# The sign of the weights from ScalarE's scaling, and their scale from Gram products: one change to an attention and FFN kernel

## The chip, the cores and the metric

The kernel runs on one NeuronCore of one Trainium2 chip. The metric is the device time of one execution in microseconds (us), lower is better; the time given is the median of three runs. Engines are named as in the profile: PE is TensorE (PEld its weight loads), DVE VectorE, ACT ScalarE, POOL GpSimd, SP SyncE, which issues all transfers here.

## What is computed

The reference takes eight batches of eight heads through a local attention (512 positions with a window of 32 to either side, plus 32 global keys and queries), then through a block that mixes with a two-dimensional Fourier transform, normalises, and applies two weight matrices with a ReLU between them:

```python
x = attention(q_l, k_l, v_l, q_g, k_g, v_g)      # 8 x 544 x 512, fp32
X = np.fft.fft(np.fft.fft(x, axis=1), axis=2)
u = x + np.real(X)
un = (u - mean(u)) / np.sqrt(var(u) + 1e-06)
ch = np.maximum(un @ w_ch1, 0.0) @ w_ch2          # 512 x 2048 and 2048 x 512, float64
return (u + ch).astype(np.float32)
```

## The kernel before

Everything in fp32 accuracy is done on PE as three fp16 products of a high and a low part. Work is cut into jobs: each of the 32 head pairs of the attention (four pairs to a batch, four units of 128 query rows to a pair), a Fourier stage for each of eight batches, 17 chunks of 256 rows for the two matrix products, of which the last four run as two pairs with seven products in place of eight. A list scheduler at the foot of the file gives each job an engine, an estimated duration, what it reads and writes, and a due time; among the jobs that are ready on an engine the one due first goes first, and the order so found is written out as fixed instruction streams. Nothing is reordered on the chip. The constants at the head of the file (`T0`, `STEP`, `U_AT`, `S2_AT`, `L_HOLD`, `BOOST` and so on) set the due times, holds and margins of that scheduler, and hence only the order.

The head of the program, some 135 us, holds three things at a time. The first is the weights: 32 blocks of 128 x 512 float64 values (k = 0 for the first matrix, k = 1 for the second, 512 KB each) are loaded and turned to fp32 by integer arithmetic on the two words of each value. `w_low` (L424 on POOL, every fourth on ACT, L422) takes the low word to mantissa bits; `w_split64` (L415, ACT) scales the high word by 2^-112 into PSUM, with buffers for two blocks; `w_size` (L428, DVE) shifts that left by three and joins it with the low bits, which loses the sign; `w_sum` (L438, PE) multiplies the size, taken as bf16, by a matrix of equal constants to sum up sizes by column; `w_sign` (L442, DVE) goes over the block again and joins the sign bit from PSUM. For every four blocks `w_max` (L448 and small operations at L533, L536, L454 to L457, DVE) makes a power-of-two scale from the largest sum. Then `w_hi` (L478, ACT) and `w_lo` (L471, DVE) write the scaled fp16 parts. The second thing is batch 0's attention: scores (L623, PE), masked minimum (L631, DVE), exponential (L638, ACT; L707 for the global queries), high part (L642, ACT), low part (L647, POOL), a transposing transfer `ph` to `pl` (L652, issued on SP), the values (L668 and L671, PE), the norm (L682 to L684, DVE). Batch 1's loads (L510, L514) follow on SP. The third is batch 0's Fourier stage and first normalisation: L830 to L855, L913, L933, L948, L965, L974, L1013 to L1056. Then the first product (`f_first`, L1084) of chunk 0 starts, which waits by its dependence `wend` for the last `w_sum` as well, and the second (`f_second`, L1103), which needs the scaled second matrix. From there chunks run while the attention of the next batches is prepared beside them.

## Time and profile before

| | us |
|---|---|
| median of three runs | 1009.96 (1007.2 to 1011.59) |
| span of the profiled execution, first to last instruction | 1005.8 |
| PE busy | 917.0 (91%) |
| DVE busy | 753.8 (75%) |
| ACT busy | 629.3 (63%) |
| POOL busy | 581.8 (58%) |

The profiled execution's own time is not listed apart from its span; the three runs are. The span lies 4.2 us under their median and 1.4 us under the fastest, and that remainder is what lies around the span. Busy times are unions over an engine's instructions, so 91% for PE is a mean over a head in which PE mostly waits and a long stretch in which it never does.

### The profile page before, as it was taken

How to read it: one execution, taken by the hardware profiler on the slowest of the kernel's cores; microseconds unless marked ns; L12 is line 12 of the kernel's file. 1: busy time of each engine (PE TensorE's matmuls, PEld its weight loads, DVE VectorE, ACT ScalarE, POOL GpSimd, SP SyncE). 2: the span in 40 equal slices, each digit the busy share in tenths (PEclk: the TensorE clock that was granted, in tenths of full speed). 3: DMA queues.
4: the chain of work that ended last, by engine and by line, in shares of the span. 5: the costliest groups of instructions: out<-in, count | busy, mean ns of one | idle time of the engine just before them, and what ended most of it. 6: DMA issues, size and time to landing. Idle time of an engine off the chain costs nothing.

```text
span 1005.8 us, 25354 instructions
## 1 busy us (share of the span) xinstructions
PE 917.0 (91%) x9784; PEld 644.1 (64%) x9784; DVE 753.8 (75%) x1928; ACT 629.3 (63%) x1361; POOL 581.8 (58%) x861
## 2 busy tenths in 40 slices
PE   1555479999999999999999999999999999999996
PEld 0344366766677677777767677777767766666663
DVE  5998898889858965887678687678775897854543
ACT  6996779976796588857677786676563545411210
POOL 5697378675595478637844774486456199910000
PEclk9999979999999999999999999999999999999998
DMA  9899348626664285537544772574263132201001
GB/s 364 260 241 198 136 110 165 119 96 116 137 153 109 66 178 131 129 60 156 128 86 97 149 159 58 108 131 98 57 122 57 43 72 54 41 8 42 1 2 42
DMA packets 225973, 112.61 MB, mean 112 GB/s; under 512 B 200860, under 2 KB 208444, under 8 KB 225852
## 3 DMA queue, kind: packets, MB, share of 16 engines
q1 hardware_dynamic: 225852, 110.99, 49.0%
q8 instruction: 76, 1.25, 0.5%
q14 instruction: 45, 0.37, 0.1%
HBM read 47.40 MB, written 9.44 MB: 57 GB/s over the span
## 4 chain that ended last, share of the span: by engine, by line
PE 76%; DVE 6%; ACT 1%; issue 1%; DVEq 0%; ACTq 0%
PE acc L1103 24%; PE ps L1084 24%; PE bk L1235 6%; PE ps L1302 4%; PE acc L1302 4%; PE bk L623 4%; PE bk L668 2%; PE bk L671 2%; PE bk L948 2%; PE bk L913 1%; PE bk L695 1%; PE bk L731 1%; DVE xt L985 1%; PE ps L1235 1%; DVE wh L471 1%
## 5 line engine op out<-in xcount | busy, mean ns | idle before, releaser
L1084 PE MATMUL ps<-uh,wh 128*128 128x256 f16 x2496 | 290.2, 274 | 0.4 <-DVE h L1093 0.4
L1103 PE MATMUL acc<-wh,h 128*128 128x512 f16 x1248 | 286.2, 379 | 0.9 <-DVE wh L471 0.7
L1084 PEld LDWEIGHTS <-wh 128*128 128x128 f16 x2496 | 241.2, 98 | 36.7 <-issue 1.3
L1103 PEld LDWEIGHTS <-h 128*128 128x128 f16 x1248 | 117.5, 98 | 128.0 <-issue 1.8
L647 POOL TENSOR_TENSOR ph<-pe,ph 128x448 f16<-128x448 f32 (+1 forms) x128 | 140.7, 1108 | 73.8 <-ACT ph L642 63.1
L1093 DVE SCALAR_TENSOR_TENSOR h<-ps,h 128x512 f16<-128x512 f32 x104 | 71.6, 688 | 87.4 <-ACT h L1089 86.8
L638 ACT ACTIVATE pe<-pe,nm 128x224 f32<-128x224 f32 (+1 forms) x256 | 107.0, 476 | 24.6 <-DVE nm L631 24.3
L1089 ACT ACTIVATE h<-ps 128x512 f16<-128x512 f32 x104 | 61.7, 593 | 89.8 <-PE ps L1084 87.9
L631 DVE CUSTOM_DVE_ANT_0 pe<-bk,msk,z 128x224 f32<-128x224 f32 (+1 forms) x256 | 102.2, 455 | 5.5 <-PE bk L623 5.4
L642 ACT ACTIVATE ph<-pe 128x448 f16<-128x448 f32 (+1 forms) x128 | 73.0, 581 | 8.1 <-DMA pl<-ph 5.9
L668 PE MATMUL bk<-vN,pl 128*128 128x65 f16 x768 | 66.6, 200 | 11.1 <-DMA pl<-ph 11.1
L668 PEld LDWEIGHTS <-pl 128*128 128x128 f16 x768 | 58.7, 102 | 19.2 <-DMA pl<-ph 12.8
L623 PEld LDWEIGHTS <-qT 64*128 64x128 f16 x1536 | 51.0, 98 | 15.8 <-issue 12.8
L623 PE MATMUL bk<-kT,qT 64*128 64x192 f16 (+2 forms) x1536 | 58.1, 221 | 2.9 <-DVE X L684 1.0
L671 PEld LDWEIGHTS <-pl 96*128 96x128 f16 (+1 forms) x768 | 56.7, 102 | 4.7
L438 PE MATMUL wl<-wm,partb 128*128 128x256 bf16 x64 | 18.9, 396 | 44.4 <-DVE wm L428 44.4
L582 POOL TENSOR_TENSOR vN<-vf,vN 128x640 f16<-128x640 f32 x32 | 46.1, 1442 | 21.5 <-ACT vN L578 14.0
L571 POOL TENSOR_TENSOR vf<-vf,z 128x640 f32<-128x640 f32 x32 | 40.8, 1275 | 26.3 <-DVE ge L533 16.2
L607 POOL TENSOR_TENSOR kT<-qk,kT 128x559 f16<-128x559 f32 x32 | 41.6, 1299 | 18.5 <-ACT kT L602 18.2
L1284 ACT ACTIVATE hb<-ph 128x512 f16<-128x512 f32 x16 | 10.1, 631 | 66.4 <-DVE ph L1269 66.4
L671 PE MATMUL bk<-vB,pl 96*128 96x65 f16 (+1 forms) x576 | 50.9, 200 | 0.0
L592 ACT ACTIVATE qk<-qk,z 128x559 f32<-128x559 f32 x64 | 44.3, 728 | 5.4 <-DVE z L533 5.4
(260 smaller groups left out, 1869.3 us busy)
## 6 DMA issues: line engine op xcount, KB each, us to landing
qk<-in_qk SPq DMA_DIRECT2D x32, 535.5 KB, 4.4
rw<-in_moe_w_ch SPq DMA_DIRECT2D x22, 512.0 KB, 6.0
vf<-in_v SPq DMA_DIRECT2D x32, 320.0 KB, 3.2
out<-X SPq DMA_DIRECT2D x13, 512.0 KB, 3.2
raw<-in_moe_w_ch SPq DMA_DIRECT2D x10, 512.0 KB, 4.7
vB<-vN SPq DMA_DIRECT2D x32, 97.5 KB, 2.1
vB<-vN SPq DMA_DIRECT2D x64, 32.5 KB, 1.9
pl<-ph SPq DMA_TRANSPOSE x128, 3.2
```

Source lines behind the costliest of these rows:

```text
L623: nc.tensor.matmul(S[h][:, t + w0:t + w1], qT[r, a, j], kT[r, k0:k0 + w1 - w0], start=m == 0, stop=m == 2)
L631: nc.vector.tensor_tensor_reduce(self.per[j][:, h, 0:w], S[h][:, t:t + w], self.msk[:, j, 0:w], z[:, 8:9], 3e38, op0=ALU.add, op1=ALU.min, ...
L638: self.nc.scalar.activation(pe[:, h], pe[:, h], AF.Exp, bias=nm[:, h:h + 1], scale=-1.0)
L642: self.nc.scalar.activation(ph[:, 0, :, 0:WIDE[i % 4]], self.per[i % 4][:, :, 0:WIDE[i % 4]], AF.Copy)
L647: self.nc.gpsimd.tensor_sub(ph[:, 1, :, 0:w], self.per[i % 4][:, :, 0:w], ph[:, 0, :, 0:w])
L668: nc.tensor.matmul(pv[:, j % 2, h], pl[:, 4 * a + 2 * h], vN[:, j, c, h, :], start=m == 0, stop=False)
L671: nc.tensor.matmul(pv[:, j % 2, h], pl[0:n, 4 * a + 2 * h + 1], vb, start=False, stop=m == 2)
L1084: nc.tensor.matmul(ps[:, q], wt[:, w, c0:c0 + P], uh[:, :, 4 * a + kt, :], start=n == 0, stop=n == 11)
L1093: self.nc.vector.scalar_tensor_tensor(h[:, 1], self.fps.pop((c, fp)), 0.0, h[:, 0], op0=ALU.max, op1=ALU.subtract)
L1103: nc.tensor.matmul(self.acc_f[c][j], h[:, a, q, j * P:(j + 1) * P], self.w[1, f][:, w, :], start=f == 0 and a == 0 and w == 0, stop=f == 1 ...
L1235: nc.tensor.matmul(ps, w[x], a[:, :, k * y + o + kt, :], start=m == 0, stop=m == 5)
L1302: nc.tensor.matmul(self.acc_f[c][j], h[:, a, q, j * P:(j + 1) * P], self.w[1, f][:, w, :], start=first and q + a + w == 0, stop=last and q ...
```

## The change

`w_split64` uses the parametric ReLU with slope -2^32 for negative inputs in place of a copy. A negative high word comes out positive and 2^32 times as large, which adds 32 to its exponent field; after `w_size`'s shift by three that bit stands where the sign belongs. So `w_size` gives the signed value and `w_sign` is gone. The sum of sizes no longer works on signed values, so `w_sum` forms Gram products: each block's four 128-column parts are both the stationary and the moving operand, and the diagonal of the 128 x 128 result holds sums of squares. `w_max` takes the row maximum of 128 columns in place of 256, a new job `w_norm` adds it over partitions by an fp32 product on PE, and a new job `w_scale` makes the power of two by an integer reciprocal root, for every group of four blocks of both matrices. The constants of the scheduler are changed as well.

```diff
+RSQRT = float(0x5F3759DF + (math.log2(600.0) - 6.5) * 2 ** 23)
-T0 = 130.0
-STEP = 5.25
+T0 = 126.448
+STEP = 5.316
-U_AT, U_PACE = 12.0, 4.0
+U_AT, U_PACE = 12.846, 3.951
-W_AT, W_PACE = 4.0, 2.2
-W2_AT, W2_PACE = 54.0, 2.0
-S_AT, S_PACE = 40.0, 3.6
-S2_AT, S2_PACE = 190.0, 3.0
-LDM = 0.8
+W_AT, W_PACE = 4.136, 2.2
+W2_AT, W2_PACE = 54.0, 2.04
+S_AT, S_PACE = 39.185, 3.504
+S2_AT, S2_PACE = 184.602, 2.329
+LDM = 0.778
-PEM, PEM0, SPM = 0.9, 0.6, 0.2
+PEM, PEM0, SPM = 0.737, 0.718, 0.205
-L_HOLD = 70.0
-QUEUE = 2.0
-LOOK_BY = 35.0
-LN, LN1, LN2 = 45.0, 20.0, 50.0
+L_HOLD = 77.65
+QUEUE = 1.933
+LOOK_BY = 31.266
+LN, LN1, LN2 = 41.656, 17.202, 49.261
-PL = 45.0
-T_AT, T_PACE = 800.0, 9.0
-BOOST = 20.0
-BOOST0 = 90.0
+PL = 34.52
+T_AT, T_PACE = 799.979, 10.217
+BOOST = 34.224
+BOOST0 = 82.708
...
-        act.activation(m, self.raw.pop((k, i))[:, :, 1].bitcast(F32), AF.Copy, scale=2.0 ** -112)
+        act.activation(m, self.raw.pop((k, i))[:, :, 1].bitcast(F32), AF.Prelu, scale=2.0 ** -112, alpha=-2.0 ** 32)
...
-            self.wl[k, c] = self.ps.tile([P, 512], F32, name="wl", tag=f"acc{c % 2}")[:, 0:256]
-        b = self.w[k, i].bitcast(BF16).rearrange("p (o n t) -> p o n t", o=2, t=2)
-        for o in range(2):
-            self.nc.tensor.matmul(self.wl[k, c], self.partb, b[:, o, :, 1], start=n + o == 0, stop=n + o == 4)
-
-    def w_sign(self, k, i):
-        w, m = self.wv.pop((k, i))
-        self.nc.vector.scalar_tensor_tensor(w, m.bitcast(I32), -0x80000000, w, op0=ALU.bitwise_and, op1=ALU.bitwise_or)
-        self.w[k, i] = w.bitcast(F32)
+            self.wl[k, c] = self.ps.tile([P, 512], F32, name="wl", tag=f"acc{c % 2}")
+        b = self.w[k, i].bitcast(BF16).rearrange("p (o n t) -> p o n t", o=4, t=2)
+        for o in range(4):
+            self.nc.tensor.matmul(self.wl[k, c][:, 0:P], b[:, o, :, 1], b[:, o, :, 1], start=n + o == 0, stop=n + o == 6)
 
     def w_max(self, k, c):
-        nc, m, w = self.nc, self.mx2, self.wsc
-        v = m[:, c:c + 1]
-        nc.vector.tensor_reduce(v, self.wl.pop((k, c)), axis=EX, op=ALU.max)
-        if k == 0:
-            self.scale_of(w[:, 4 + c:5 + c], v)
-            self.twice_inv(w[:, c:c + 1], w[:, 4 + c:5 + c])
-        elif c == 3:
-            v = m[:, 4:5]
-            nc.vector.scalar_tensor_tensor(m[:, 0:4], m[:, 0:4], 2.0 ** -5, w[:, 0:4], op0=ALU.mult, op1=ALU.mult)
-            nc.vector.tensor_reduce(v, m[:, 0:4], axis=EX, op=ALU.max)
+        self.nc.vector.tensor_reduce(self.mx2[:, 4 * k + c:4 * k + c + 1], self.wl[k, c][:, 0:P], axis=EX, op=ALU.max)
+
+    def w_norm(self, k, c):
+        self.nc.tensor.matmul(self.wl[k, c][:, P:P + 1], self.part, self.mx2[:, 4 * k + c:4 * k + c + 1], start=True, stop=True)
+
+    def w_scale(self, k, c):
+        ve, m, w = self.nc.vector, self.mx2, self.wsc
+        v, r = self.wl.pop((k, c))[:, P:P + 1].bitcast(I32), (w[:, 4 + c:5 + c] if k == 0 else m[:, 4 + c:5 + c])
+        ve.tensor_scalar(r.bitcast(I32), v, -0.5, RSQRT, op0=ALU.mult, op1=ALU.add)
+        ve.tensor_scalar(r.bitcast(I32), r.bitcast(I32), EXPO, None, op0=ALU.bitwise_and)
+        self.twice_inv(w[:, c:c + 1] if k == 0 else r, r)
+        if k and c == 3:
+            v, m = m[:, 8:9], m[:, 4:8]
+            ve.scalar_tensor_tensor(m, m, 2.0 ** -5, w[:, 0:4], op0=ALU.mult, op1=ALU.mult)
+            ve.tensor_reduce(v, m, axis=EX, op=ALU.max)
             self.scale_of(w[:, 13:14], v)
-            nc.vector.tensor_scalar_mul(w[:, 8:12], w[:, 0:4], w[:, 13:14])
+            ve.tensor_scalar_mul(w[:, 8:12], w[:, 0:4], w[:, 13:14])
             self.twice_inv(w[:, 14:15], w[:, 13:14])
...
-            add("DVE", .66, self.w_sign, k, i, r=[m, w], w=[w], t=T + 2)
             if t % 4 == 3:
                 d = [("ws", 0, x) for x in range(4)] + [("ws", 1, x) for x in range(3)] if (k, c) == (1, 3) else []
-                add("DVE", .65 if k == 0 else .35 if c < 3 else 1.25, self.w_max, k, c, r=[wl] + d, w=[("ws", k, c)], t=T + 6)
+                wm = ("wm", k, c)
+                add("DVE", .27, self.w_max, k, c, r=[wl], w=[wm], t=T + 5)
+                add("PE", .3, self.w_norm, k, c, r=[wm], w=[wl], t=T + 5.5)
+                add("DVE", .5 if c < 3 or k == 0 else 1.4, self.w_scale, k, c, r=[wl] + d, w=[("ws", k, c)], t=T + 6)
```

## Rows read from the trace of the kernel before

**Rows 1.** The page: busy tenths in 40 slices of 25 us, by engine.
```profile
PE   1555479999999999999999999999999999999996
DVE  5998898889858965887678687678775897854543
```
**Rows 2.** Windows by stage: busy us (instructions) by engine, granted clock, DMA share, GB/s.
```profile
20.00:77.00 57.00, 29.63 (x375) 20.33 (x373) 54.21 (x133) 54.75 (x111) 46.45 (x55) 1.00 0.91 262
77.00:107.00 30.00, 14.47 (x214) 10.17 (x210) 25.59 (x64) 19.41 (x47) 20.39 (x28) 1.00 1.02 235
107.00:136.00 29.00, 13.15 (x128) 10.14 (x128) 26.65 (x70) 22.85 (x48) 12.46 (x27) 0.81 0.23 76
136.00:176.00 40.00, 38.92 (x480) 28.88 (x478) 35.85 (x92) 33.44 (x70) 32.69 (x42) 0.96 0.69 147
176.00:800.00 624.00, 622.41 (x7272) 444.22 (x7269) 479.88 (x1305) 432.24 (x955) 386.99 (x585) 1.00 0.54 111
800.00:996.00 196.00, 195.24 (x1317) 128.57 (x1315) 122.60 (x241) 55.52 (x110) 73.20 (x106) 1.00 0.13 31
...
200.00:300.00 100.00, 98.65 (x1192) 69.83 (x1191) 81.47 (x219) 76.61 (x173) 71.00 (x110) 1.00 0.56 125
```
**Rows 3.** Windows of L442 (`w_sign`) alone: DVE busy us (instructions), clock, DMA share, GB/s.
```profile
20.00:77.00 57.00, 12.51 (x19) 1.00 0.91 262
77.00:107.00 30.00, 5.47 (x9) 1.00 1.02 235
```
**Rows 4.** Groups of 0 to 150 us: busy us, mean ns | idle before, releaser.
```profile
L438 PE MATMUL wl<-wm,partb 128*128 128x256 bf16 x64 | 18.9, 396 | 44.4 <-DVE wm L428 44.4
L448 DVE TENSOR_REDUCE mx<-wl 128x1 f32<-128x256 f32 x8 | 3.3, 413 | 0.0
L533 DVE TENSOR_SCALAR wsc<-mx 128x1 int32<-128x1 int32 x5 | 0.8, 154 | 0.2
L478 ACT ACTIVATE wh<-wm,wsc 128x512 f16<-128x512 f32 x18 | 12.4, 713 | 1.8 <-DVE wsc L533 1.0 <-DVE wsc L457 0.8
```
**Rows 5.** L415 (`w_split64`): duration ns min/median/max, first and last start.
```profile
L415 ACT ACTIVATE ps<-rw x22: 592/612/640, 7.1 to 102.5; 128x512 f32<-128x512 f32 x22
L415 ACT ACT_TABLE_LOAD  x1: 1283/1283/1283, 0.7 to 0.7; - x1
```
**Rows 6.** Waits from 20 to 107 us: total us, times, longest.
```profile
PE wl L438 <- DVE wm L428: 27.4, 14, 3.9
PE bk L668 <- DMA pl<-ph: 11.1, 4, 4.9
ACT ps L415 <- DVE wm L442: 3.9, 3, 2.0
```
**Rows 7.** Timeline of SP, 98 to 101 us: start, us, instruction.
```profile
98.33 0.42 SPq L510 DMA_DIRECT2D qk<-in_qk  x1
98.91 1.23 SPq L652 DMA_TRANSPOSE pl<-ph  x1
```
**Rows 8.** Timeline of DVE, 118 to 121 us.
```profile
118.84 0.69 DVE L442 SCALAR_TENSOR_TENSOR wm<-ps,wm 128x512 int32<-128x512 int32 x1
120.68 0.47 DVE L933 SCALAR_TENSOR_TENSOR z<-bk,z 128x288 f16<-128x288 f32 x1
```
**Rows 9.** Timeline of PE: batch 0's last values, its Fourier stage, first product.
```profile
104.54 0.24 PE L668 MATMUL bk<-vN,pl 128*128 128x65 f16 x1
121.21 0.35 PE L948 MATMUL bk<-c2r,z 128*128 128x129 f16 x3 [1.07 <-DVE z L933]
135.38 7.07 PE L1084 MATMUL ps<-uh,wh 128*128 128x256 f16 x48
```
**Rows 10.** Timeline of ACT: first and last change between exponentials and splits.
```profile
33.13 0.89 ACT L638 ACTIVATE pe<-pe,nm 128x256 f32<-128x256 f32 x2
88.85 0.61 ACT L415 ACTIVATE ps<-raw 128x512 f32<-128x512 f32 x1
```
**Rows 11.** The page's list of transfers: issues, median us to landing.
```profile
pl<-ph SPq DMA_TRANSPOSE x128, 3.2
```

More of the change, by code (lines that the diff above doesn't have):

```diff
@@ L351, in __init__ @@
         self.pg = c.tile([P, 544], F32, name="pg")
-        self.mx2 = c.tile([P, 5], F32, name="mx2")
+        self.mx2 = c.tile([P, 9], F32, name="mx2")
         self.wsc = c.tile([P, 15], F32, name="wsc")
@@ L426, in w_size @@
     def w_size(self, k, i):
-        (w, m), t = self.wv[k, i], self.wt.pop((k, i))
+        (w, m), t = self.wv.pop((k, i)), self.wt.pop((k, i))
         self.nc.vector.scalar_tensor_tensor(w, m.bitcast(I32), 3, t, op0=ALU.logical_shift_left, op1=ALU.bitwise_or)
```

## The prediction, made before the result was known

> **What bounds the kernel now.** I read the slices of the page first, then windows cut at the changes they show, then the waits and timelines inside the head. The slices show PE filled from the seventh or eighth slice to the last, and DVE and DMA filled before that [rows 1]. The windows put numbers on it: from 136 to 996 us PE is busy 38.92 of 40, 622.41 of 624 and 195.24 of 196 us, so it loses 3.4 us in 860 [rows 2]. That stretch is PE's own work, none of which the change touches. It starts when chunk 0's first product starts, at 135.38 [rows 9]. So the end moves one for one with that start, and whatever the change does elsewhere is free.
>
> In front of it the bound changes. From 20 to 77 us DVE is busy 54.21 and ACT 54.75 of 57 us, with the DMA engines at 0.91; from 77 to 107 the DMA share is 1.02 while ACT falls to 19.41 of 30 and PE waits 11.1 us for transposed probabilities [rows 2, 6]; from 107 to 136 DVE is busy 26.65 of 29 us in batch 0's Fourier stage and normalisation, and DMA is at 0.23. The change takes work from DVE alone, so the question for each stage is who is late next.
>
> **The change part by part.** *The pass removed.* `w_sign` is busy 12.51 us from 20 to 77 (19 blocks), 5.47 from 77 to 107 (9) and 0.69 after that (1), 18.7 us in all [rows 3, 8]; the first three blocks lie earlier, where no engine is full. *Small operations added:* four groups of the first matrix go from two to three, three of the second from none to three, the last from five to eight: 4 + 9 + 3 = 16, at 0.154 us each [rows 4] 2.5 us. The eight maxima read 128 columns less; estimated at half of 413 ns at most, they give back 8 x 0.2 = 1.6 us at most, and I take 1.0. Net on DVE: 18.7 - 2.5 + 1.0 = 17.2 us, of 106.5 us busy between 20 and 136. It is not 17 us off the path:
>
> A. *Batch 0's attention, up to its last values at 104.54* [rows 9]. From 77 on the transfers decide, and the change moves no bytes: that bound gives 0. What DVE can buy is that loads and transposes are asked for earlier, into the gaps of 20 to 77, where DMA is idle 9% of 57 us = 5.1 us. The last transpose, issued at 98.91 behind batch 1's load at 98.33 [rows 7], is used at 104.54, 5.6 us later; the median landing is 3.2 [rows 11], so 2.4 us more if that load stands behind it (`L_HOLD` is put 7.65 later). Bounds 0 and -7.5. ACT is the other hurdle, with 2.25 us idle in those 57; but 3.9 us of its waits are for `w_sign` to free a PSUM buffer [rows 6] and go, and its `w_hi`, 18 before 150 us at 0.71 [rows 4], can give way, since nothing needs them before 135. I take -5.1, the room in the DMA row.
>
> B. *The Fourier stage.* The last `w_sign` and the last maximum with its small operations stand in DVE's queue from 118.84 to 120.68, before the step PE waits 1.07 us for [rows 8, 9]. With blocks finished earlier they leave: -1.8, at worst 0.
>
> C. *Second product.* PE idles 1.1 us between 136 and 176 [rows 2], where `w_lo` of the second matrix is due. Their scale comes sooner: -0.5, between 0 and -1.1.
>
> D. *Gram products.* 64 products of 256 columns become 128 of 128, each with its own weight load, and 8 fp32 ones come. No row shows them. The old pair costs under 0.8 us (2 x 396 ns, unpipelined) [rows 4]; the new four by the same mean cost up to 1.6, so up to 32 x 0.8 = 26 us more PE time in the worst case, and none in the best, as columns are equal. PE works 57 of the 116 us from 20 to 136 and waits 27.4 us for DVE before this very line [rows 2, 6], which hides them; if that cover fails, see the rival. The new wait is `w_norm`'s for `w_max`: behind it in PE's order stand scores and values. With the small operations I charge +0.3, between 0 and +2.5.
>
> E. *The other function on ACT.* No row has it. The copy takes 612 ns; the same 512 columns with one more operand in memory (`w_hi`, its scale) take 713 [rows 4, 5]. Bounds 0 and 32 x 0.1 = +3.2; below zero is excluded, since the columns read and written stay. I take 0: both numbers it is given are constants, as the copy's are.
>
> F. *Due times.* They reorder and neither add nor remove work. Gain: at most the 2.35 us PE idles from 176 to 996. Loss: if each 100 us became as loose as the loosest (1.35 us idle, 200 to 300 [rows 2]), 8.2 x 1.35 - 2.35 = +8.7. I take 0, as PE's row is full with the old ones and nothing in the new ones is large against the 109 us of a batch.
>
> Sum: -5.1 - 1.8 - 0.5 + 0.3 = -7.1 us, on the span 1005.8 - 7.1 = 998.7. The median of the runs lies 4.2 above the profiled span, which I add: **1002.9 us**.
>
> **A rule that speaks against the change.** The row shows one table load, 1283 ns at 0.7 us, for a whole program that uses copy, absolute value, square, identity, ReLU and exponential on ACT [rows 5]. The Trainium skill, "ScalarE activation tables: per-element evaluation and per-set limits", section "What a function is on this engine", says that two functions in different sets are one such load apart, and that with the same operands the instruction costs the same; "ScalarE: Activation LUTs", section "Table sets: the hidden batching unit", lists cheap functions that every set carries and does not name the parametric one. By the second half of the first rule E is 0; by its first half there is a rival, below. No run yet shows which.
>
> **The rivals.** *1. The transfers hold.* DMA at 1.02 from 77 to 107 [rows 2] is full whatever DVE does, and the weights' 16 MB come through it first. Then A is 0 and B, C and D stay: -2.0, 1008.0 us. For it: PE's waits there name `pl`. Against it: 0.91 before 77 leaves room.
>
> *2. The engines were all that mattered.* DVE sets when transfers are asked for, and the head shrinks until ACT, whose 97.0 us of work from 20 to 136 are the next largest, is as full as DVE was (92%): 97.0/0.92 = 105.5 in place of 116, -10.5, 999.5 us. Against it: the DMA share again.
>
> *3. Slower: PE's queue blocks on the new product.* PE takes its instructions in order. The wait before `w_sum` was 27.4 us in 14 times, 2.0 us each [rows 6]; it did not matter, because scores were placed around it. `w_norm` adds eight waits for DVE, which runs late whenever `w_lo` is slow. If each costs batch 0's chain 2.0 us, that is 16: -7.1 + 16 = +8.9, 1018.9 us. It decides from the fourth of eight waits on the chain (4 x 2.0 = 8.0, over the 7.1 gained); six give more than 0.5%. Against it: PE idles 59 of those 116 us. The loose due times of F (+8.7) would end in the same place.
>
> *4. The function sits in another table set.* ACT's timeline changes between exponentials and splits 20 times between 33.13 and 88.85 [rows 10], on an engine without slack up to 77. 20 x 1.283 = 25.7 us: -7.1 + 25.7 = +18.6, 1028.6 us. For it: no row has the function. Against it: six functions needed no second load.
>
> **How the numbers follow.** Forecast 0.50, rival 1 0.23, rival 2 0.10, rival 3 0.12, rival 4 0.05. A measurement of this kernel tells about 0.5%, 5 us, from no change, so faster means under 1004.9. Of the forecast's 0.50 I put 0.43 under that line and 0.07 over it, as its bounds in A straddle it; with all of rival 2 that is 0.53. Same: 0.07 + rival 1's 0.23 + a weak rival 3, 0.02 = 0.32. Slower: 0.10 + 0.05 = 0.15. The range goes down to A, B and C at their ends and half of F's gain (-7.5 - 1.8 - 1.1 - 1.2 + 0.3 = -11.3, with 2 us of spread among runs: 996.5) and up over rival 1 with E's +3.2 (1011.5); left out are most of rivals 3 and 4 and a little at the low end.
>
> **What would show it.** L415 at 612 ns and one table load: E right, rival 4 dead. Batch 0's last values near 99.5 in place of 104.54, and the first L1084 near 128.5: A and B right; values still at 104 with a DMA share of 1: rival 1. PE idle before the new fp32 product of 2 us each with scores behind it: rival 3. PE from its first product to its last still taking about 861 us: F is 0; longer, the due times cost. The prediction is wrong if DVE's 17 us are gone and the first L1084 starts where it did, or if it starts sooner and the last product does not.

## The result, and the profile after

| us | before | after |
|---|---|---|
| median of four runs each, taken together | 1009.37 (1007.2 to 1011.59) | 1016.98 (1014.29 to 1018.74) |
| span of the profiled execution | 1005.8 | 1015.5 |
| PE busy | 917.0 | 924.4 |
| DVE busy | 753.8 | 732.5 |
| ACT busy | 629.3 | 627.9 |
| start of chunk 0's first product | 135.38 | 133.92 |
| end of the last product | 996.2 | 1005.9 |

The change makes the kernel slower, by 0.8%: the ratio after to before is 1.0084, 95% interval 1.0057 to 1.011. The forecast was 1002.9. VectorE lost 21 us of busy time, the first product starts 1.5 us sooner, and the end comes 9.7 us later in the traces. The medians differ by 7.6 only, because the profiled execution of before is its fastest one (median 3.6 above its span) and that of after is close to its median (1.5 above).

The windows of after, to be set beside [rows 2] (us; busy us and instructions of PE, PEld, DVE, ACT, POOL; granted clock; DMA share; GB/s):

```profile
20.00:77.00 57.00, 28.41 (x394) 21.86 (x395) 42.66 (x114) 54.62 (x110) 48.70 (x54) 0.64 0.93 265
77.00:107.00 30.00, 16.15 (x264) 13.58 (x262) 22.60 (x67) 19.63 (x50) 20.18 (x30) 0.56 1.02 210
107.00:136.00 29.00, 16.61 (x132) 12.59 (x132) 26.53 (x71) 22.79 (x49) 12.96 (x27) 0.50 0.28 96
136.00:176.00 40.00, 37.66 (x456) 27.59 (x454) 36.21 (x91) 33.95 (x70) 31.07 (x41) 0.93 0.78 150
...
136.00:996.00 860.00, 849.14 (x9003) 597.21 (x9001) 628.59 (x1623) 518.24 (x1130) 490.85 (x731) 0.99 0.46 93
```

From 20 to 77 us DVE fell from 54.21 to 42.66, as it should. ACT (54.62) and DMA (0.93) stayed where they were. The loss is in the last row. From 136 to 996 PE is busy 849.14 us where before's three rows add to 856.57, so it waits 10.9 us in place of 3.4.

The clock column of the head is not to be set beside [rows 2]. The first clock record of before lies at 118 us, and ahead of it the view shows 1.00. But its values products last as long there as after's do, which stand at 0.56 to 0.64, and less from 182 us on (duration ns min/median/max, first and last start; before, before later, after):

```profile
L668 PE MATMUL bk<-vN,pl x96: 233/244/259, 47.8 to 105.1; 128*128 128x65 f16 x96
L668 PE MATMUL bk<-vN,pl x624: 190/193/204, 182.4 to 772.8; 128*128 128x65 f16 x156
L669 PE MATMUL bk<-vN,pl x96: 191/243/259, 46.2 to 104.1; 128*128 128x65 f16 x96
```

So both heads run for the most part at the lower level, 1.2 GHz, and these durations show no difference between them.

What PE waited for from 140 to 1000 us in after (us in total, times, longest):

```profile
PE acc L1104 <- DVE h L1094: 3.4, 2, 1.8
PE acc L1104 <- DVE wh L472: 2.2, 1, 2.2
PE bk L914 <- DVE z L934: 1.7, 1, 1.7
PE bk L463 <- ACT junk L528: 1.4, 1, 1.4
PE bk L624 <- DVE nm L632: 0.8, 1, 0.8
PE bk L914 <- DVE nm L632: 0.7, 1, 0.7
PE bk L463 <- DVE xt L989: 0.5, 1, 0.5
```

All but one are waits for DVE, the engine that lost work. Behind two of these places the clock also falls. The window before and the one with the wait for L472, then the next (same columns):

```profile
168.00:172.00 4.00, 1.84 (x9) 0.78 (x8) 4.00 (x3) 1.99 (x5) 2.44 (x3) 1.00 0.93 232
172.00:176.00 4.00, 4.00 (x23) 1.91 (x21) 3.43 (x10) 3.65 (x8) 1.09 (x1) 0.57 1.17 167
176.00:180.00 4.00, 4.00 (x51) 2.41 (x49) 2.49 (x9) 2.94 (x7) 2.40 (x5) 1.00 0.83 155
```

After PE stood for 2.16 us, 3.4 us (172.3 to 175.7) are granted at 0.5, which is 1.2 GHz of 2.4; the same comes at 366.9 to 370.3, after waits of 0.48 and 0.78. Before has neither. Behind the waits of 1.56 to 1.80 us at 315, 417 and 590 it does not come, and what decides is not shown. At half the rate each loses 1.7 us, and 0.4 more goes at the start, where after runs 4.3 us of products at 0.5 and before 3.4. So the 9.7 us close: -1.5 (start) + 7.4 (waits) + 3.8 (clock).

Two smaller readings. The new function on ACT and the table loads (duration ns min/median/max, first and last start), beside [rows 5]:

```profile
L416 ACT ACTIVATE ps<-rw x22: 596/614/638, 4.5 to 99.9; 128x512 f32<-128x512 f32 x22
L416 ACT ACT_TABLE_LOAD  x1: 1283/1283/1283, 0.7 to 0.7; - x1
```

And the new products, the fp32 product and the new maximum (first two: groups of 0 to 150 us with busy us, mean ns, idle time before; third: ns min/median/max), beside [rows 4]:

```profile
L439 PE MATMUL wl<-wm 128*128 128x128 bf16 x128 | 18.2, 288 | 43.7 <-DVE wm L429 42.1 <-DVE mx L450 1.1 <-DVE wsc L450 0.4
L445 PE MATMUL wl<-mx,part 128*128 128x1 f32 x16 | 4.1, 323 | 1.2 <-DVE mx L442 1.2
L442 DVE TENSOR_REDUCE mx<-wl x8: 273/282/292, 14.5 to 103.8; 128x1 f32<-128x128 f32 x8
```

### The profile page after: what moved, and what is told of

The parts are those of the page before. It is cut to its first block, busy times and chain, and to the rows that moved or that the text cites. A ratio compares the mean times of both kernels' runs of the same rounds, so it can differ in the third digit from the quotient of the medians.

```text
span 1015.5 us, 25506 instructions
## 1 busy us (share of the span) xinstructions
PE 924.4 (91%) x9864; PEld 653.2 (64%) x9864; DVE 732.5 (72%) x1912; ACT 627.9 (62%) x1361; POOL 582.0 (57%) x861
## 4 chain that ended last, share of the span: by engine, by line
PE 73%; DVE 8%; ACT 2%; issue 1%; POOL 0%; DVEq 0%; ACTq 0%; POOLq 0%
PE ps L1085 23%; PE acc L1104 22%; PE bk L1236 7%; PE ps L1303 4%; PE acc L1303 4%; PE bk L624 3%; PE bk L669 2%; PE bk L672 2%; PE bk L949 1%; PE bk L914 1%; DVE pe L632 1%; PE bk L696 1%; DVE xt L986 1%; PE bk L732 1%; DVE h L1094 1%
## 5 line engine op out<-in xcount | busy, mean ns | idle before, releaser
L1104 PEld LDWEIGHTS <-h 128*128 128x128 f16 x1248 | 117.6, 98 | 133.8 <-DVE h L1094 4.3
L1094 DVE SCALAR_TENSOR_TENSOR h<-ps,h 128x512 f16<-128x512 f32 x104 | 71.6, 688 | 100.9 <-ACT h L1090 99.2
L632 DVE CUSTOM_DVE_ANT_0 pe<-bk,msk,z 128x224 f32<-128x224 f32 (+1 forms) x256 | 102.3, 453 | 10.3 <-PE bk L624 10.0
L1065 POOL TENSOR_TENSOR ve<-ve 128x2 f32<-128x2 f32 x17 | 9.4, 555 | 85.3 <-DVE unh L1037 35.0
L572 POOL TENSOR_TENSOR vf<-vf,z 128x640 f32<-128x640 f32 x32 | 41.6, 1300 | 28.7 <-DVE ge L534 14.7
L439 PE MATMUL wl<-wm 128*128 128x128 bf16 x128 | 18.2, 288 | 43.7 <-DVE wm L429 42.1
L608 POOL TENSOR_TENSOR kT<-qk,kT 128x559 f16<-128x559 f32 x32 | 41.3, 1290 | 17.7 <-ACT kT L603 14.7
```

The lines of the kernel that those rows point to most:

```text
L632: nc.vector.tensor_tensor_reduce(self.per[j][:, h, 0:w], S[h][:, t:t + w], self.msk[:, j, 0:w], z[:, 8:9], 3e38, op0=ALU.add, op1=ALU.min, ...
L1094: self.nc.vector.scalar_tensor_tensor(h[:, 1], self.fps.pop((c, fp)), 0.0, h[:, 0], op0=ALU.max, op1=ALU.subtract)
L1104: nc.tensor.matmul(self.acc_f[c][j], h[:, a, q, j * P:(j + 1) * P], self.w[1, f][:, w, :], start=f == 0 and a == 0 and w == 0, stop=f == 1 ...
```

## Experiments: which part of the change costs

The change has two halves that can be set apart: the new structure (split, Gram products, scale) and the new numbers that the planner orders by.

**e1_structure_only.** The changed kernel with all due times of before:

```diff
-T0 = 126.448
-STEP = 5.316
+T0 = 130.0
+STEP = 5.25
...
-BOOST0 = 82.708
+BOOST0 = 90.0
```

> The new sign, the Gram products and the new scale, with all due times, holds and margins of the kernel before. Theory 1 (the structure gives a little and the new due times cost PE idle and half-clock time after the first product has started): about 1007 us, between 1004 and 1010, the first product at 132 to 134 us, PE idle between the first product and the last under 4.5 us. Rival 2 (the structure itself, through the lists it leads to, loosens the long stretch): 1014 to 1019, PE idle there near the 10.9 us of the changed kernel.

Measured: 1006.44 against 1009.65, ratio 0.9969 [0.9956, 0.9982]. The first product starts at 134.4 (0.4 later than theory 1 has it), PE waits 3.3 us after it, and the last product ends at 994.8.

**e2_due_times_only.** The kernel before with all new due times (the same lines the other way round).

> The kernel before with its second VectorE pass and column sums, and all due times of the changed one. Theory 1: the loss comes without the structure too, so 1016 to 1021 us, with PE idle of 8 us or more after the first product. Rival 2: about 1009 us, PE idle near 3.4.

Measured: 1016.61, ratio 1.007 [1.0046, 1.0095]. The first product starts at 141.2 and PE waits 7.4 us after it. So the structure gains 3.2 us, and the due times cost about 7 us in the old structure and 10.5 in the new one (1016.98 against 1006.44). The loss is the numbers', not the new instructions'. But it is not the same loss: in the old structure 5.8 us of it come ahead of the first product (141.2 against 135.4), and the waits behind it are 7.4 us, a little under the 8 that theory 1 asked for.

**Which numbers.** Groups of them were put back, or put in alone. All but T0 and STEP, LN, PL, T_AT and BOOST belong to the head or to the planner's margins.

e3_late_old: the changed kernel with T0, STEP, PEM, LOOK_BY, LN, PL, T_AT and BOOST old.

> The changed kernel with the due times of the long stretch put back (T0, STEP, the three LN, PL, T_AT, BOOST, and the margins PEM and LOOK_BY); those of the head (U, W, S, LDM, L_HOLD, QUEUE, BOOST0) stay new. Theory 1 in the form that the stretch's own due times cost: 1005 to 1010 us. In the form that those of the head do: 1014 to 1019. Rival 2: 1014 to 1019.

e4_head_old: the changed kernel with U_AT, W_AT, W2_AT, S_AT, S2_AT, LDM, L_HOLD, QUEUE and BOOST0 old.

> The changed kernel with the due times of the head put back and those of the long stretch new, the counterpart of the run before. Theory 1, the stretch's own: 1014 to 1019 us. The head's: 1005 to 1010. Rival 2: 1014 to 1019. If both halves lie between 1009 and 1014, the loss has no single owner.

g1_ln, g2_step, g3_boost: e1 with one group new each.

```diff
-LN, LN1, LN2 = 45.0, 20.0, 50.0
+LN, LN1, LN2 = 41.656, 17.202, 49.261
...
-T0 = 130.0
-STEP = 5.25
+T0 = 126.448
+STEP = 5.316
...
-PL = 45.0
-T_AT, T_PACE = 800.0, 9.0
-BOOST = 20.0
+PL = 34.52
+T_AT, T_PACE = 799.979, 10.217
+BOOST = 34.224
```

> New structure, old due times, but the three LN new (the normalisation of a chunk, and the last parts of a batch's Fourier stage, due 3 us later or sooner). Theory C (the loss is where DVE's and POOL's steps fall beside each other, so any change of the lists may bring some of it): between 1006 and 1015 us, with the excess of DVE's operations between 140 and 800 us and PE idle higher than the 69 and 3.3 us of the old due times where the time is higher. Rival G (one group of due times carries the loss): two of these three runs within 2 us of 1006.4, the third at 1014 or more.

> The same with T0 and STEP new instead: the chunks due 3.6 us sooner and spaced 1.3% wider. Theory C: between 1006 and 1015 us. Rival G: within 2 us of 1006.4, or the one at 1014 or more; the chunks' own spacing is the likeliest owner.

> The same with PL, T_AT, T_PACE and BOOST new instead: the last batch's Fourier stage due 14 us sooner and the last chunks' mixes later. The loss of the changed kernel lies before 650 us, so under both theories less than 3 us over 1006.4; PE idle before 600 us as with the old due times.

h2_after_step_old: the changed kernel with T0 and STEP alone old. h3_ln_boost: e1 with the groups of g1 and g3 new together.

> The changed kernel whole, with the old T0 and STEP (due times of the products in the long stretch) alone put back. Theory A: those two numbers own the loss after the first product by themselves, as they did when set alone in the new structure (+7.8 us): TensorE idles 3 to 4 us after its first product in place of 10.9, time 1006 to 1008. Rival B: any of several new numbers is enough to loosen the order; idle stays over 7 us and the time at 1013 or more. Between the two: they interact.

> The new structure with the old due times, but LN, LN1, LN2, PL, T_AT, T_PACE and BOOST new: the two groups that took 1.1 and 1.0 us off singly. If their effects were due to themselves and add: 1004.3. If what an order costs is not a sum over the numbers that made it: anything from 1003 to 1015, with the first product between 132 and 136 and TensorE's idle time after it saying which half moved.

| kernel | us | ratio to before | first product | PE waits after it |
|---|---|---|---|---|
| before | 1009.4 | | 135.4 | 3.4 |
| after | 1016.98 | 1.0084 [1.0057, 1.011] | 133.9 | 10.9 |
| e1 structure only | 1006.44 | 0.9969 [0.9956, 0.9982] | 134.4 | 3.3 |
| e3 late numbers old | 1011.83 | 1.0023 [1.0008, 1.0037] | 137.7 | 4.2 |
| e4 head's numbers old | 1017.96 | 1.0084 [1.0059, 1.0108] | 133.3 | 14.0 |
| g1 LN new | 1005.34 | 0.9954 [0.994, 0.9969] | 132.1 | 3.0 |
| g2 T0, STEP new | 1014.27 | 1.0042 [1.0026, 1.0059] | 135.1 | 8.0 |
| g3 PL, T_AT, BOOST new | 1005.41 | 0.9964 [0.9946, 0.9983] | 135.2 | 2.3 |
| h2 T0, STEP old | 1015.74 | 1.0059 [1.0038, 1.008] | 138.5 | 7.1 |
| h3 LN, PL, T_AT, BOOST new | 1006.10 | 0.9961 [0.9941, 0.9981] | 132.6 | 4.2 |

T0 and STEP alone cost 7.8 us (g2), which made them look like the owner. Put back in the full set they give 1.2 us, inside the intervals, and the idle time is still 7.1 (h2): the reading that they own the loss fell. The times can't tell whether the gains of g1 and g3 add in h3, since their sum, 1004.3, lies inside its interval; by its trace h3 has g1's early first product (132.6) and not g3's few waits (4.2). So a set of numbers has no price of its own. It selects one of many orders, and the order has the price.

What is common to after, e4, g2 and h2 is PE waiting 7 to 14 us after its first product, nearly all of it for DVE. e2, e3 and h2 lose ahead of that product as well (141.2, 137.7, 138.5). In g2 the waits are in the main a single one of 6.3 us at 246.8, with DVE's operations in front of it at their usual durations (L975 four times in 1.65 us) but for one (L1022, 1.19 us): there it is the queue's order that does it.

## Experiment: what makes after's order lose

In after it is something else. DVE and then POOL around one of the waits for L1094 (start us, us, instruction):

```profile
583.28 1.57 DVE L844 TENSOR_TENSOR e<-e 128x258 f32<-128x258 f32 x1
584.77 1.47 DVE L845 TENSOR_TENSOR e<-e 128x256 f32<-128x256 f32 x1
586.16 1.37 DVE L821 TENSOR_TENSOR s<-s 128x256 f32<-128x256 f32 x1
587.57 1.23 DVE L822 TENSOR_TENSOR s<-s 128x128 f32<-128x128 f32 x1
588.72 0.75 DVE L823 TENSOR_TENSOR s<-s 128x128 f32<-128x128 f32 x1
589.40 0.68 DVE L1094 SCALAR_TENSOR_TENSOR h<-ps,h 128x512 f16<-128x512 f32 x1
```

```profile
582.69 1.88 POOL L583 TENSOR_TENSOR vN<-vf,vN 128x640 f16<-128x640 f32 x1
584.53 1.43 POOL L608 TENSOR_TENSOR kT<-qk,kT 128x559 f16<-128x559 f32 x1
585.92 1.34 POOL L608 TENSOR_TENSOR qT<-qk,qT 128x512 f16<-128x512 f32 x1
587.22 1.43 POOL L572 TENSOR_TENSOR vf<-vf,z 128x640 f32<-128x640 f32 x1
588.61 0.71 POOL L500 TENSOR_TENSOR gT<-gn,gT 128x256 f16<-128x256 f32 x1
```

Each of DVE's five operations ends 0.15 to 0.3 us after one of POOL's. At 313.82 the last three take 0.41, 0.29 and 0.28 us. L1094, which PE waits 1.8 us for, stands behind them. The wait for L472 is of the same kind: two of them take 4.99 us from 166.66, where two take 1.41 in h8 at 105.37, and POOL is busy without a gap from 163.67 to 170.4.

**e8_light_pool.** After's order, with POOL's work on batches from the third on cut:

```diff
-        self.mul(s["vf"], s["sc"])
+        self.mul(s["vf"] if p < 8 else s["vf"][:, 0:1], s["sc"])
...
-        self.nc.gpsimd.tensor_sub(vN[:, :, 1, :, 0:64], self.st[p]["vf"], vN[:, :, 0, :, 0:64])
+        j = 5 if p < 8 else 1
+        self.nc.gpsimd.tensor_sub(vN[:, 0:j, 1, :, 0:64], self.st[p]["vf"][:, 0:j], vN[:, 0:j, 0, :, 0:64])
...
-        w = WIDE[i % 4]
+        w = WIDE[i % 4] if i < 32 else 64
```

> The changed kernel, order and due times kept, with POOL's work from the third batch on cut: its subtractions for the low parts of v, k and the probabilities and its scaling of v touch only a part of their columns, so those values are wrong. Theory C (with the new due times DVE's operations with two SBUF inputs stand beside POOL's, each held until POOL's ends, and the product's own DVE step comes late behind them): the excess of DVE's operations over their usual duration from 140 to 800 us falls from 78 to under 35 us, PE idle after the first product from 10.9 to under 6, the time to 1007 to 1012. Rival D (the new due times put DVE's steps too late whatever their duration): PE idle stays over 8.5 and the time within 2 us of 1017.

Measured: 1005.77, ratio 0.9969 [0.9955, 0.9983], 11 us under after in the same order; the values that these parts make are wrong in this kernel. The window from 136 to 996 (columns as above), beside after's last row there:

```profile
136.00:996.00 860.00, 855.69 (x9055) 600.72 (x9053) 592.51 (x1634) 520.51 (x1132) 366.33 (x730) 1.00 0.46 94
```

POOL's busy time fell from 490.85 to 366.33 us, and DVE's from 628.59 to 592.51 although no DVE instruction was touched. PE waits 2.4 us after its first product; 2.2 of that is the wait for L472, which lies in a batch whose work was left. Theory C holds and rival D falls: most of after's waits are DVE operations held while POOL works. Its figures were too cautious for the time (1007 to 1012) and too bold for the holding: 36 us less DVE time leave about 42 of the 78 us of excess, where it asked for under 35. The Trainium skill, "SBUF — State Buffer", section "Who interferes with whom", says that a DVE instruction with two inputs in SBUF contends with a GpSimd instruction that reads SBUF, and calls the port pair that they share an exclusive lock; the rows from 583 to 589 agree, 0.42 us becoming 1.57.

The holding is in every order, and DVE is busy for no longer in after than in before: from 136 to 996 us it is 638.33 us in before, 628.59 in after and 621.83 in e1. The eight L844 and L845 (in before L843 and L844) last, in ns min/median/max, in before, in e1 and in after:

```profile
L843 DVE TENSOR_TENSOR e<-e x8: 414/679/1573, 110.7 to 784.0; 128x258 f32<-128x258 f32 x8
L844 DVE TENSOR_TENSOR e<-e x8: 413/676/1573, 111.1 to 784.4; 128x256 f32<-128x256 f32 x8
```

```profile
L844 DVE TENSOR_TENSOR e<-e x8: 415/495/1148, 109.6 to 774.6; 128x258 f32<-128x258 f32 x8
L845 DVE TENSOR_TENSOR e<-e x8: 413/422/1574, 110.1 to 774.9; 128x256 f32<-128x256 f32 x8
```

```profile
L844 DVE TENSOR_TENSOR e<-e x8: 415/1027/1572, 109.3 to 782.9; 128x258 f32<-128x258 f32 x8
L845 DVE TENSOR_TENSOR e<-e x8: 414/964/1472, 109.8 to 783.2; 128x256 f32<-128x256 f32 x8
```

All three have single operations of 1.1 to 1.6 us. But in after the median is 1.0: in four of the eight batches (at 214, 309, 583 and 682 us) both operations last 1.25 us or more, which happens in no batch of before and e1, and at 583 L1094 stands behind them. So where the holding falls seems to count for more than how much of it there is; no run moved it alone. Which order escapes is not to be read from the numbers that made it.

## Experiments: where the head's gain went

In e1's order, with the due times out of the way, 17 us less DVE work gave 1.0 us at the first product. Four kernels keep that order and change one load each.

**f1_pass_back**: a second DVE pass of the old size after each split, with its result unused in value.

```diff
+        self.nc.vector.scalar_tensor_tensor(w, m.bitcast(I32), -0x80000000, w, op0=ALU.bitwise_and, op1=ALU.bitwise_or)
```

> The run e1_structure_only (new structure, old due times, first product at 134.4 us, 1006.4 us) with the order of every queue kept, and the second VectorE pass added again behind each w_size, where it changes no value: 32 more operations of 0.68 us, 22 us. Theory A (before the first product ACT and the transfers end last, and DVE's pass was beside them): the first product moves by 3 us at most, to 137.5 or sooner, and the time is 1006 to 1010. Rival B (DVE sets the head, and the gain was given back by the order): the first product at 144 us or later, 1015 us or more.

**f2_split_twice**: ACT's split done twice.

```diff
+        act.activation(m, self.raw[k, i][:, :, 1].bitcast(F32), AF.Prelu, scale=2.0 ** -112, alpha=-2.0 ** 32)
```

> The same run, order kept, with w_split64 done twice into the same place: 32 more ACT operations of 0.61 us, 19.6 us, some 12 of them between 20 and 77 us where ACT is busy 55.87 of 57. Theory A with ACT as the bound: the first product moves by 8 us or more, to 142 or later. With the transfers as the bound: by 3 us at most. Rival B: by 3 us at most.

**f3_half_loads**: half the bytes of 16 of the 32 weight blocks; the other half of their columns is wrong.

```diff
-        self.nc.sync.dma_start(raw.rearrange("p n t -> p (n t)"), self.w_src(k, i).bitcast(I32))
+        half = n > 7 and kind != "uh"
+        to, src = raw.rearrange("p n t -> p (n t)"), self.w_src(k, i).bitcast(I32)
+        self.nc.sync.dma_start(*((to[:, 0:512], src[:, 0:512]) if half else (to, src)))
```

> The same run, order kept; 16 of the 32 weight blocks load half of their bytes, so half of their columns hold values of an earlier block. 4.2 MB less, 11.6 us at the 363 GB/s of the first 25 us. Theory A with the transfers as the bound: the first product 3 us or more sooner, 131.4 or before. With ACT as the bound: within 1.5 us of 134.4. Rival B: within 1.5 us.

**f4_light_act**: less ACT work before 107 us (busy 83.59 us in place of e1's 89.67); parts of batch 0's high values are left out. One of its three edits:

```diff
...
-        self.nc.scalar.activation(ph[:, 0, :, 0:WIDE[i % 4]], self.per[i % 4][:, :, 0:WIDE[i % 4]], AF.Copy)
+        w = WIDE[i % 4] if i > 15 else 32
+        self.nc.scalar.activation(ph[:, 0, :, 0:w], self.per[i % 4][:, :, 0:w], AF.Copy)
```

> The run e1_structure_only with its order kept and ACT's work for batch 0's attention cut by about 7 us: the high parts of its probabilities, of its keys and of two pairs' values cover only a part of their columns, so those values are wrong. Theory E (with DVE's pass gone ACT ends last in the head): the first product 3 us or more sooner than 134.4, 131.4 or before, 1003 us or less. Rival F (with the pass gone the head is a chain through all engines, where a lighter engine gives little and a heavier one costs): 133 us or later.

Measured: f1 1022.2, ratio 1.0134 [1.0119, 1.0149], first product 150.5 (+16.1 for 21.8 us of work); f2 1023.08 in a single run, 149.1 (+14.7 for 19.6 us); f3 1005.81 in a single run, 133.6 (-0.8); f4 1005.77 in a single run, 134.4 (0). Rival B had f1 right, the theory that DVE had become free did not; for f2 it was the other way round, since rival B asked for 3 us at most and ACT as the bound for 8 or more. For f4 rival F holds and theory E fell. An engine made heavier in a fixed order costs about three quarters of its added work here, and an engine or the transfers made lighter give 0.8 us or nothing. That fits a chain through all of them, so I looked for that chain.

Its last links stand in the timelines. In before, POOL and ACT in front of the first product of the Fourier stage:

```profile
100.82 0.29 POOL L757 COPY xt<-X 32x128 f32<-32x128 f32 x1 [1.58 <-DVE X L684]
106.43 0.72 POOL L875 TENSOR_TENSOR st<-xt 32x255 f32<-32x255 f32 x1 [0.93 <-DVE wm L428]
110.14 0.45 POOL L881 TENSOR_TENSOR et<-st 32x128 f32<-32x128 f32 x1
110.90 1.47 ACT L886 ACTIVATE ht<-et,dsc 32x513 f16<-32x513 f32 x2 [0.22 <-DVE dsc L536]
```

In e1 the same four, one line number on, and the transfer that the second of them waits for:

```profile
102.06 0.71 POOL L758 COPY xt<-X 32x128 f32<-32x128 f32 x1 [5.36 <-DVE X L685]
104.01 0.58 SPq L764 DMA_DIRECT2D xt<-xd  x1
106.47 0.72 POOL L876 TENSOR_TENSOR st<-xt 32x255 f32<-32x255 f32 x1 [1.26 <-DMA xt<-xd]
110.49 0.64 POOL L882 TENSOR_TENSOR et<-st 32x128 f32<-32x128 f32 x1
111.16 1.47 ACT L887 ACTIVATE ht<-et,dsc 32x513 f16<-32x513 f32 x2 [0.30 <-POOL et L882]
```

Two chains meet at L887. One goes through batch 0's last norm and the Fourier scale `dsc`; it came 4 us sooner (the norm ends at 103.4 in place of 107.2, `dsc` at 106.4 in place of 110.6). The other goes through the norm before the last, `x_tail` on POOL, two row swaps of 1 KB (`x_mid`) and `d_tail` on POOL. It did not move: `d_tail` starts at 106.47 in place of 106.43 and L887 at 111.16 in place of 110.90. In before `d_tail` had two conditions that ended together. The swap arrived at 106.3; the one that came last, by its row, is a `w_size` (L428), because `d_tail` writes into a buffer that held a block's low words:

```profile
105.76 0.68 DVE L428 SCALAR_TENSOR_TENSOR wm<-ps,lw 128x512 int32<-128x512 int32 x1
```

In e1 the weights are through by then and the swap alone is left. In e2 that `w_size` comes far later than the swap, and POOL stands 12.1 us for it:

```profile
114.21 0.72 POOL L875 TENSOR_TENSOR st<-xt 32x255 f32<-32x255 f32 x1 [12.13 <-DVE wm L428]
```

L886 then starts at 118.5 there; how much of e2's late first product hangs on this no run shows.

In e1 the norm of this second chain even ends later, 101.9 in place of 100.7, because PE has the values for it behind the last `w_sum` and the new `w_norm`, and DVE has it behind the new small operations (99.70 to 101.1). From the first Fourier product on, the distance to chunk 0's first product is 21.0 us in e1 and 21.1 in before (113.4 to 134.4, 114.3 to 135.4).

**h5_scale_later** tests the small operations alone. After the order is made, the last `w_scale` and what needs it are moved behind batch 0's last norm:

```diff
         plan.run()
+        o = plan.order
+        x = next(j for j in o if j.fn.__name__ == "w_scale" and j.a == (1, 3))
+        y = [j for j in o if j.fn.__name__ == "norm" and j.a[0] < 8][-1]
...
+        o[:] = [j for j in o[:n] if j not in late] + late + o[n:]
```

> The new structure in the old due times' order, with one group moved by hand after the order was made: the three-step scale of the last weight group (w_scale, eight small VectorE operations) and the four weight splits that need it go behind batch 0's last norm; everything else stays in place. Without the edit the norms start at 101.04 and 102.53 and the first product at 134.4. Theory A: those small operations are what kept the head's gain from the end; the first product comes 1.5 to 2.3 us sooner, time about 1004.5. Rival B: TensorE's values are the later condition (they start at 99.5, behind the fp32 product, and end at 101.66), so the norms move by 0.3 and 0.8 us at most, the first product by under 1.0, time 1005.4 to 1006.4.

**h8_batch0_first** moves everything that stands in front of batch 0's chain, in three queues; **h9_ln_batch0_first** is the same on g1's order:

```diff
+        behind([get("d_even", (0, 0))], get("masked", (15,)))
+        behind([get("d_odd", (0, 0))], get("p_lo", (15,)))
+        behind([get("w_sum", (1, 14))], get("norm", (7,)))
```

> The new structure in the old due times' order, and nothing made lighter: by hand, batch 0's attention goes ahead of what stands between it and the front of each queue. Its last three p_lo on GpSimd (92.96 in the trace without the edit) go ahead of the first d_odd (89.87 to 93.0), its last two masked ahead of the first d_even, its last values ahead of the last two w_sum and the w_norm (TensorE waits 3.48 us for those at 97.49 with the values behind them), its last norms ahead of the last w_max and w_scale. Theory A: the head is bound by the order in which batch 0's chain passes the queues, not by any engine's or the transfers' load; transposes are asked for up to 3 us sooner, the last values end at 98.5 to 100 in place of 101.7, the first product starts at 131 to 133 in place of 134.4, time 1003.5 to 1005. Rival B: transfers hold; the last values still end after 101 and the first product stays within 0.7 us. Rival C: what was put back (d_even, d_odd, the last weights' sizes) is needed just as soon, so that the first product starts later than 134.4.

> The same edit by hand on the order that the new LN, LN1, LN2 give with the other due times old (1005.34 us, first product 132.1 without the edit). Theory A as for h8_batch0_first: the first product 1 to 2 us sooner, time 1003.5 to 1004.5. Rival B and C: 1005 to 1007.

**h6_all_light** is h5 with the edits of f3 and f4 on top.

> As h5_scale_later, with two resources lightened at once on top: 4.2 MB fewer weight bytes loaded, some 7 us less ScalarE work before 107 us (high halves of batch 0's probabilities, keys and values partly not written), so part of the computation is left out. Singly these moved the first product from 134.4 by -0.8 and 0. Theory A: transfers and ScalarE end together in front of that product, so that only both at once give: 130 or sooner. Rival B: neither bounds it, batch 0's own chain of waits does; 132 to 134, no more than the single effects added.

| kernel | us | norm before the last, last norm end | second row swap issued, `d_tail` starts | L887 starts | first product |
|---|---|---|---|---|---|
| before | 1009.4 | 100.7, 107.2 | 102.3, 106.4 | 110.9 | 135.4 |
| e1 | 1006.44 | 101.9, 103.4 | 104.0, 106.5 | 111.2 | 134.4 |
| f3 | 1005.81 (single run) | 101.2, 102.6 | 103.2, 105.2 | 110.1 | 133.6 |
| f4 | 1005.77 (single run) | 100.5, 102.2 | 102.5, 106.6 | 111.0 | 134.4 |
| h5 | 1006.91, 0.9971 [0.9959, 0.9983] | 101.2, 103.2 | 102.9, 107.8 | 112.4 | 135.7 |
| h6 | 1009.32 (single run) | 101.6, 102.9 | 103.2, 106.9 | 112.2 | 135.5 |
| h8 | 1007.09, 0.9968 [0.9956, 0.998] | 101.5, 102.3 | 103.2, 106.8 | 112.5 | 135.6 |
| g1 | 1005.34, 0.9954 [0.994, 0.9969] | 97.1, 103.9 | 99.8, 101.6 | 107.7 | 132.1 |
| h9 | 1006.30, 0.9964 [0.995, 0.9978] | 95.7, 102.3 | 100.1, 102.0 | 109.0 | 133.8 |

None of the four hand edits gained; theory A fell in all of them. In h5 the norms moved by 0.7 and 0.2 us, near rival B's 0.3 and 0.8; the first product came 1.3 later in the trace, and the timed runs can't tell h5, h8 and e1 apart. In h6 the two lighter loads together gave no more than singly (135.5 against h5's 135.7). In h9 the last norm ends 1.6 us sooner than in g1, and L887 starts 1.4 later. In h8 rival C is what the trace shows: the last norm ends 1.1 us sooner, and yet everything behind it is later. ACT in h8:

```profile
104.62 1.33 ACT L479 ACTIVATE wh<-wm,wsc 128x512 f16<-128x512 f32 x2 [1.41 <-DVE wsc L458]
105.86 0.40 ACT L792 ACTIVATE junk<-X 128x256 f16<-128x256 f32 x1
...
112.48 1.47 ACT L887 ACTIVATE ht<-et,dsc 32x513 f16<-32x513 f32 x2
```

The two weight splits that I had put back now wait for the moved scale, in front of the square sum that the Fourier scale needs (L792, ready since the norm at 102.3); and the sums of the next batches, in front of L887 in ACT's queue, move back with it. Clearing one queue had filled another.

The table shows what the row swap does. From its issue to `d_tail`'s start it takes 1.9 us in g1, 2.0 in f3, 2.5 in e1, 3.6 to 4.1 in h6, h8 and f4 and 4.9 in h5, for 1 KB. In e1, f4, h5, h6 and h8 `d_tail` starts between 106.5 and 107.8 whether it was issued at 102.5 or at 104.0. Loads of the next batches are issued just ahead of it (98 to 101), and in the window from 101 to 107 the DMA share is 0.84 to 0.98 in those five and 0.79 in f3; in g1 those loads are issued behind the swap, from 100.4. That the swap waits behind those loads fits all these numbers, but no run took those loads away and left the rest, so it is not shown.

g1, and h9 which is built on it, are the orders of the table where the norm before the last and the swap come early (97.1 and 99.8 in g1). `d_tail` then ends at 105.5 in g1, off the path; L887 waits for the last norm's chain instead, and the first product is at 132.1. That is the gain that e1 left lying, 2.3 us of it.

## Why the prediction was wrong, by its own steps

**F, the due times: the step that failed.** They were taken at 0, with a bound of +8.7; they cost about 10.5 us (after against e1). The reason given, that PE's row is full with the old ones and nothing in the new ones is large against a batch, does not carry: a shift of 0.066 in STEP and 3.6 in T0 cost 7.8 us (g2), while shifts of 10 and 14 in PL and BOOST cost nothing (g3). A numerically small change can reorder all the queues. What the runs show in place of the 0 is PE waiting for DVE 10.9 us in place of 3.4, most of it behind DVE operations that POOL holds (e8 takes 11 us off in the same order). The bound took looseness as idle time alone, 1.35 us per 100, and had no term for the clock, which gave 3.8 of the 9.7. The upper end of the range holds nothing of this step: it is rival 1 with E's +3.2 (1008.0 + 3.2 = 1011.2, written as 1011.5; the low end comes to 996.7, written as 996.5), and the result passes it by 5.5. Nor does F's bound end where rival 3 does, as the prediction has it: -7.1 + 8.7 gives 1011.6, and rival 3 gives 1018.9. That 1016.98 lies near rival 3's time is luck, since its mechanism is not what made it.

**A, batch 0's attention: half right.** At its own milestone it held in e1: the last values end 3.7 us sooner (105.4 to 101.7), the last norm 3.8, against -5.1. The failed step is the next one, that the end moves with it: the row tail's chain through `x_mid` ended within half a microsecond of it and was not in the prediction; of its two conditions in before the removed pass eases one, the `w_size` in DVE's queue, and not the other, the swap. With after's own due times the norm gains 1.8 only, and the first product 1.5.

**B, the Fourier stage: wrong.** The first Fourier product to the first L1084 takes 21.1 us in before, 21.0 in e1 and 22.0 in after. The 1.8 us of `w_sign` and the maximum in DVE's queue were not what that stage waited for.

**C, second product: right in e1, turned round in after.** PE waits 0.2 us from 136 to 176 in e1, against 1.1. In after it waits 2.2 for the same `w_lo`, held by POOL.

**D, Gram products: right in size, missed in place.** They cost PE 18.2 us against 18.9 before, so the columns, which are as many, fit the cost and the number of products does not. The small operations take 0.15 us or a little more, the maximum 0.28, the waits of `w_norm` 1.2 us in all in after. In e1 they are 5.3 us in three times, most of it one wait:

```profile
72.61 0.50 PE L445 MATMUL wl<-mx,part 128*128 128x1 f32 x2 [4.41 <-DVE mx L442]
```

And the last group stands in front of the norm before the last, on the chain that decides (+1.2 us there).

**E and rival 4: settled.** 614 ns against 612, one table load: the other function costs nothing. The Trainium skill's rule cited for it ("ScalarE activation tables: per-element evaluation and per-set limits", section "What a function is on this engine") is borne out in its second half; no second set was needed here.

**Rivals 1 to 3.** Transfers were full from 77 to 107 as rival 1 said, but 4.2 MB fewer gave 0.8 us (f3). Rival 2's -10.5 did not come: with the due times out of the way the structure gains 3.2 (e1). Rival 3's own mechanism, waits of 2 us at each `w_norm`, did not appear in after; e1 has one long wait, and gains all the same.

**From span to median.** I added 4.2 us. In other executions 1.8 us lie around the span (1017.34 against 1015.5 in after). The other 2.4 were that the profiled execution of before was its fastest. Here that did no harm, since both sides carried it.

## What to carry to other kernels

Where a planner makes the order, a change of its numbers is a change of its own: measure it alone, and give it the range that neighbouring sets of numbers show (here 1005 to 1018 us), since its effect is neither small when the numbers are nor a sum over them. Before work is taken off a busy engine, follow every chain that ends at the next stage's first instruction, also the ones with small transfers and the idle engine in them; the second latest one bounds the gain. When an engine that lost work makes others wait more, compare the durations of single operations with their usual ones before looking at queues.

The best version run is e1 with the new LN (g1), 1005.34 us, ratio to before 0.9954 [0.994, 0.9969]; it is not told apart from g3, h3 and e1 by these runs.

## What the runs showed of the hardware

- A DVE operation with two SBUF inputs can last three to four times as long beside POOL (0.42 to 1.57 us). Over 860 us this is worth 36 us of DVE time (628.59 against 592.51 with POOL's work cut by a quarter).
- A wait of PE of 2.16 us was followed by 3.4 us at a granted clock of 0.5; h2's of 3.0 at 246.8 by the same (249.6 to 253.0); in g2, around a wait of 6.3 us at 246.8, it is 0.5 from 250.6 to 260.9. Such a wait of PE can cost more than itself, but need not: e4's of 3.0 us up to 590.9, h2's of 2.3 up to 869.0 and e1's of 2.0 up to 247.5 were followed by none.
- From the issue of a 1 KB transfer to the start of its reader it took from 1.9 us (g1) to 4.9 (h5). Loads issued ahead of it fit the difference; that they make it is not shown.
